# A hand-ordered plan changed: first products of pairs 0 and 1 for both units at once, last halves in two banks, another order of loads

## The chip, the cores and the metric

The kernel runs on one core of a Trainium2 chip. A core has TensorE (matrix products, "PE" in the profile, with its weight loads as "PEld"), VectorE (DVE), ScalarE (ACT), GpSimd (POOL) and SyncE (SP), which here only issues DMAs. The metric is the device time of one execution in microseconds (us); the time before is the median of 3 runs. A profile is one further execution, recorded by the hardware profiler.

## What is computed

A gated linear recurrence (4 batches, 8 heads, 768 steps, head size 48), whose output is at once the input of a two-layer block with SiLU:

```python
f = 1.0 / (1.0 + np.exp(-f_logit))
for t in range(S):
    state = f[:, :, t, :, None] * state + np.einsum('bhd,bhe->bhde', k[:, :, t], v[:, :, t])
    y[:, :, t] = np.einsum('bhd,bhde->bhe', q[:, :, t], state)
x = y.transpose(0, 2, 1, 3).reshape(B * S, H * D)      # 3072 x 384
h = x @ w_in                                           # 384 x 2048
g = h * (1.0 / (1.0 + np.exp(-h)))
return g @ w_out                                       # 2048 x 384
```

All inputs and the output are float32; the kernel computes its products in bf16.

## The kernel before

The 768 steps of a batch are cut into 6 chunks of 128. A *unit* is one chunk of one batch, with all its heads; there are 24. Two units make a *pair*, and there are 12 pairs. Pairs 0 to 3 (form "T") hold the chunks 0 and 1 of one batch, with even and odd steps in the two units; pairs 4 to 11 (form "N") hold the same chunk of two batches.

The program has no loops in the usual sense. PLAN (from line 37) is a list of words, and the last loop (line 510) runs through them and calls `emit`. A word reads `kind.pair.unit...:engine:buffers`. It is put on the queue of the engine named (A ScalarE, V VectorE, G GpSimd, S SyncE, P TensorE). Each engine takes its own words in the order of PLAN and waits, word for word, for what the word needs. So PLAN sets the order on every engine and which buffer is used: PSUM has 8 banks (the number behind P).

The kinds, in the order in which a pair goes through them:

- `f`, `k`, `q`, `v`: loads of the inputs on SyncE's queue (line 241). For T pairs a load has 384 KB; pair 0's f comes in two halves.
- `E`, `L`: exponential and logarithm on ScalarE, together the logarithm of the gate (lines 248, 260, 263). `cs`: its running sum, as a product with a triangle of ones (lines 324, 331).
- `ia`, `a`, `al`: exponentials of that sum (lines 336, 338, 278). `ki`, `qg`: k and q times these (line 341). `vb`: v in bf16 (line 185 or 187).
- `tq`, `qkc`: transposes of q and k on TensorE (line 348) and the copy out of PSUM; later pairs do it with a DMA, `qkD` (line 360).
- `sc`, `at`: the products of q and k within a chunk (lines 369, 373) and the mask over them (line 377).
- `d`, `sd`, `su`: the new state (lines 297, 406, 410, 420). `y`, `yi`: the output of the recurrence (lines 285, 385, 389), `yc` its copy, `yT` with `xc`, or `yD`, its transpose (lines 397, 401).
- `mi.P.j`: two of 16 blocks of 128 columns of the first product for pair P, h = x @ w_in, 6 matmuls (line 271). With a third number only one unit's 128 columns of x are taken, without it both units' 256. `si.P.j`: SiLU of the block on ScalarE (line 276), into hT.
- `mo.P.i.n`: a quarter of the second product for unit i, 4 matmuls of 384 columns (line 306); with a fourth number only one half of the 384 output columns. `oc`: copy out of PSUM. `so`: store (lines 316, 318).
- `wi.n`, `wo.n`: a quarter of w_in or w_out, loaded and cast by a DMA that GpSimd issues (lines 216, 219). wi.n holds the blocks j = 2n and 2n + 1.
- `idle`: matmuls on zeros without use (line 465), which keep TensorE working while it has nothing to do.

ScalarE needs one table of functions for `E`, `L`, `ia`, `a`, `al` and another for `si`; when the kind changes in PLAN, the program loads the other (line 513).

Before the plan's own order starts, its first four loads are issued (line 482), and then masks, ones and zeros are made.

Which buffer a word takes is decided by a name. For `mo` and `oc` it is the pair and the unit, so the two halves of pair 11's output lie in one bank:

```python
if kind == "mo":
    return [("o", *rest[:2])]
```

Of the kernel before, what the change touches and what calls it, by code (L numbers as in the profile page):

```python
# [49 lines left out]
mi.0.1.1:P:0 si.0.3:A:1 mi.0.1.0:P: mi.0.5.1:P: si.1.5:A: ki.3.0:G: mi.0.0.0:P:6 si.0.1:A: mi.0.6.0:P:5 mi.0.0.1:P: su.1.1:G:0 mi.0.7.1:P:4 si.0.0:A:  # L50
mi.0.7.0:P: si.0.2:A: mi.0.6.1:P: ki.3.1:G: mi.1.1.0:P: si.0.6:A: mi.1.7.0:P:0 tq.3.0:P:6 mi.1.7.1:P: qkc.3.0:A:1 mi.0.4.0:P:2 tq.3.1:P:5 si.1.7:A:
mi.0.4.1:P: f.4.0:S:1 mo.0.0.0:P:6 qkc.3.1:A: mo.0.1.0:P:0 si.1.1:A: mi.1.6.1:P:5 si.0.5:A: mi.1.6.0:P: si.1.2:A: mo.1.1.0:P:7 si.1.6:A: mo.0.1.1:P:
si.0.4:A: si.0.7:A: sc.3.1:P:3,1 sc.3.0:P:5,2 at.3.1.0:V:2 vb.2.0:A:4 mo.0.1.2:P: at.3.1.1:V: mo.1.1.1:P: at.3.0.0:V:3 mo.0.0.1:P: q.4.0:S:4
# [56 lines left out]
def kernel(  # L110
# [100 lines left out]
    def emit(kind, rest, eng):  # L211
# [91 lines left out]
        if kind == "mo":  # L303
            cols = part_of(rest[3:])
            for n in range(4 * rest[2], 4 * rest[2] + 4):
                nc.tensor.matmul(at("o", P, i)[:, cols], at("hT", P)[:, n, i * C:(i + 1) * C], w_out_sb[:, n, cols], start=(n == 0), stop=(n == NT - 1))  # L306
# [240 lines left out]
```

## Time and profile before

| | us |
|---|---|
| median of 3 runs (181.39 to 182.42) | 181.42 |
| the profiled execution | 180.93 |
| its span, first to last instruction | 179.2 |

The span is what the views of the trace cover; 1.7 us of the profiled execution lie around it. The page also gives the busy share of each engine in 40 slices of 4.5 us (in tenths, 9 is 90% or more), with what the DMA engines moved:

```profile
PE   6769989999999999999999999999999999999993
ACT  3989983895289999999967558988796991178410
DMA  6999999999999799998478998994994496320043
GB/s 159 324 325 325 240 204 207 199 187 190 242 230 212 92 208 221 168 241 144 84 145 170 188 210 141 252 263 103 179 251 94 97 190 215 88 70 0 0 150 117
```

TensorE is full from the sixth slice on. Its digits in the first five hold the matmuls on zeros too. The DMA engines are full to about 60 us. In views of groups a line reads: source line, engine, operation, output<-inputs, shapes, count | busy us, mean ns of one | idle us just before, and what ended it. In views in order of time the first number is the start, the second the length.

### The profile page before, as it was taken

The page shows a single profiled execution, that of the slowest core. Times are in us where ns is not written, and L with a number is a line of the kernel's source. Part 1 is how long each engine was busy: PE and PEld are TensorE (multiplying, and loading weights), DVE is VectorE, ACT ScalarE, POOL GpSimd, SP SyncE. Part 2 cuts the span into 40 slices and gives each one's busy share as a digit, 9 for nine tenths or more (in the row PEclk, how much of TensorE's full clock was granted, in tenths as well). Part 3 has the DMA queues.
Part 4 walks back from the last instruction along what each step waited for, and adds up shares of the span by engine and source line. Part 5 has one row for each costly group of instructions (what it writes and reads, how often), then busy time and mean ns, then how long its engine had stood idle before and what let it go on. Part 6 is the DMA issues. An engine that isn't in the chain of part 4 may idle for free.

```text
span 179.2 us, 4981 instructions
## 1 busy us (share of the span) xinstructions
PE 170.5 (95%) x2042; PEld 129.0 (72%) x2044; DVE 79.7 (44%) x166; ACT 132.7 (74%) x251; POOL 61.6 (34%) x106
## 2 busy tenths in 40 slices
PE   6769989999999999999999999999999999999993
PEld 2345779975788866778678877875876786788782
DVE  7078994008821246456673703342335747500002
ACT  3989983895289999999967558988796991178410
POOL 6036995000274004554044170636303592000010
...
DMA  6999999999999799998478998994994496320043
GB/s 159 324 325 325 240 204 207 199 187 190 242 230 212 92 208 221 168 241 144 84 145 170 188 210 141 252 263 103 179 251 94 97 190 215 88 70 0 0 150 117
...
## 3 DMA queue, kind: packets, MB, share of 16 engines
...
q14 instruction: 6, 0.05, 0.1%
...
## 4 chain that ended last, share of the span: by engine, by line
PE 77%; ACT 9%; DVE 4%; DMA 3%; SPq 2%; issue 1%; POOL 1%; DVEq 0%
PE pb L306 32%; PE pb L271 32%; ACT hT L276 4%; DMA q<-in_q_dram 3%; PE pb L373 2%; SPq L241 2%; PE pb L385 2%; PE pb L348 2%; PE pb L389 2%; DVE qk L341 2%; ACT L513 1%; DVE atm L377 1%; PE pb L331 1%; PE pb L397 1%; DVE st L420 1%
## 5 line engine op out<-in xcount | busy, mean ns | idle before, releaser
L306 PE MATMUL pb<-w_out_sb,hT 128*128 128x384 bf16 (+1 forms) x416 | 70.4, 314 | 0.2 <-ACT hT L276 0.2
L271 PE MATMUL pb<-xT,w_in_sb 128*128 128x256 bf16 (+1 forms) x672 | 68.9, 257 | 0.0
L271 PEld LDWEIGHTS <-w_in_sb 128*128 128x128 bf16 x672 | 56.6, 98 | 7.5 <-issue 0.3
L276 ACT ACTIVATE hT<-pb 128x512 bf16<-128x512 f32 x96 | 51.8, 617 | 12.4 <-PE pb L271 12.0
L306 PEld LDWEIGHTS <-hT 128*128 128x128 bf16 x416 | 37.7, 98 | 18.7 <-ACT hT L276 0.4
L377 DVE TENSOR_TENSOR atm<-pb,triu 128x512 bf16<-128x512 f32 x32 | 20.6, 684 | 20.5 <-PE pb L373 17.8
L336 ACT ACTIVATE x<-pb 128x384 f32<-128x384 f32 x48 | 22.1, 508 | 1.5 <-PE pb L331 1.4
L420 POOL TENSOR_TENSOR st<-sd,al 48x192 bf16<-48x192 f32 x32 | 16.6, 518 | 18.7 <-PE pb L385 12.1
L341 POOL TENSOR_TENSOR qk<-q,x 128x384 bf16<-128x384 f32 x11 | 11.3, 1025 | 31.9 <-ACT x L336 14.5
L513 ACT ACT_TABLE_LOAD x15 | 19.2, 1283 | 0.3
L185 ACT COPY ob<-pb 128x384 f32<-128x384 f32 (+1 forms) x15 | 6.8, 453 | 12.6 <-PE pb L306 12.6
L377 DVE TENSOR_TENSOR atm<-pb,mask 128x512 bf16<-128x512 f32 x16 | 10.2, 685 | 12.4 <-ACT hT L276 11.1
L187 DVE COPY ob<-pb 128x384 f32<-128x384 f32 (+1 forms) x11 | 5.8, 535 | 22.2 <-PE pb L306 22.2
L318 POOL DMA_DIRECT2D out_dram<-ob x8 | 4.6, 578 | 28.4 <-ACT ob L185 24.8
L316 POOL DMA_DIRECT2D out_dram<-ob x14 | 7.6, 548 | 19.6 <-DVE ob L187 15.9
L341 DVE TENSOR_TENSOR qk<-q,x 128x384 bf16<-128x384 f32 x13 | 7.6, 593 | 13.7 <-ACT x L336 13.7
L248 ACT ACTIVATE e<-f 128x768 f32<-128x768 f32 (+1 forms) x13 | 10.4, 800 | 4.4 <-DMA f<-in_f_logit_dram 4.2
L410 DVE TENSOR_TENSOR sd<-pb,st 128x384 f32<-128x384 f32 x16 | 8.9, 554 | 10.6 <-PE pb L406 3.9
L341 POOL TENSOR_TENSOR qk<-k,x 128x384 bf16<-128x384 f32 x10 | 10.8, 1082 | 6.4 <-ACT al L278 2.0
L185 ACT CAST yb<-pb 128x384 bf16<-128x384 f32 x12 | 5.6, 479 | 9.7 <-PE pb L389 9.6
L341 DVE TENSOR_TENSOR qk<-k,x 128x384 bf16<-128x384 f32 x14 | 9.9, 710 | 0.9 <-ACT x L336 0.9
L187 DVE CAST yb<-pb 128x384 bf16<-128x384 f32 x12 | 6.6, 556 | 8.0 <-PE pb L389 5.9
...
## 6 DMA issues: line engine op xcount, KB each, us to landing
...
```

Of the source, the lines that this page charges most:

```text
L185: nc.scalar.copy(dst, src)
L187: ENG[eng].tensor_copy(dst, src)
L248: return nc.scalar.activation(e, at("f", P)[:, j * w:(j + 1) * w], AF.Exp, scale=-1.0)
L271: nc.tensor.matmul(h[:, i, cols], w_in_sb[:, kk, n * 128:(n + 1) * 128], at("xT", P)[:, kk, cols], start=(kk == 0), stop=(kk == KT - 1))
L276: return nc.scalar.activation(at("hT", P)[:, 2 * j:2 * j + 2, :], at("h", P, j).rearrange("p (n c) -> p n c", n=2), AF.Silu)
L306: nc.tensor.matmul(at("o", P, i)[:, cols], at("hT", P)[:, n, i * C:(i + 1) * C], w_out_sb[:, n, cols], start=(n == 0), stop=(n == NT - 1))
L336: nc.scalar.activation(at(kind, P, i).rearrange("p h d -> p (h d)"), at("cs", P, i)[:, 0:HD], AF.Exp, scale=1.0 if kind == "ia" else -1.0)
L341: ENG[eng].tensor_mul(at("qk", P, i)[:, j, :, 0:D], heads("qk"[j], P, i), at("ia" if j else "a", P, i))
L377: ENG[eng].tensor_mul(at("atm", P, i)[:, r], at(f"s{r}", P, i).rearrange("p (n c) -> p n c", c=C), mask[:, None, :].to_broadcast([C, NP, C]))
L410: nc.vector.tensor_add(at("sd", P, i), d_ps, prev_state(P, i))
L420: ENG[eng].tensor_mul(at("st", P, i)[lo:lo + D, :, r * D:(r + 1) * D], src[lo:lo + D, :, r * D:(r + 1) * D], al_of(P, i)[lo:lo + D, :, Non ...
L513: nc.scalar.preload_act_table_set(TABLES[mode])
```

## The change

PLAN is replaced as a whole; PAIRS, SLOTS and all of the arithmetic stay. Beside it, the name under which the halves of `mo` and `oc` find their bank takes the number of the half, so that a half has a bank of its own:

```diff
@@ emit
-                nc.tensor.matmul(at("o", P, i)[:, cols], at("hT", P)[:, n, i * C:(i + 1) * C], w_out_sb[:, n, cols], start=(n == 0), stop=(n == NT - 1))
+                nc.tensor.matmul(at("o", P, i, *rest[3:])[:, cols], at("hT", P)[:, n, i * C:(i + 1) * C], w_out_sb[:, n, cols], start=(n == 0), stop=(n == NT - 1))
...
-            copy(eng, at("ob", P, i)[:, cols], at("o", P, i)[:, cols])
+            copy(eng, at("ob", P, i)[:, cols], at("o", P, i, *rest[2:])[:, cols])
@@ takes
-            return [("o", *rest[:2])]
+            return [("o", *rest[:2], *rest[3:])]
```

The start of PLAN, to a little past the first product (`mi.0.2.0`):

```diff
-f.2.0:S:0 k.0.0:S:0 f.0.1:S:1 f.0.0:S: E.2.0:A:0 f.1.0:S:2 L.2.0:A:0 v.1.0:S:0 q.0.0:S:0 idle.512.11::0 cs.2.1:P:0 E.0.1:A:1 E.0.0:A: k.1.0:S:1
-cs.2.0:P:1 L.0.1:A:1 L.0.0:A: E.1.0:A:0 q.1.0:S:1 idle.512.1::2 cs.0.0:P:2 cs.0.1:P:3 a.0.0:A:0 vb.1.1:G:0 f.3.0:S:3 L.1.0:A:2 ia.0.1:A:1 cs.1.0:P:4
-a.0.1:A:2 qg.0.0:V:0 v.0.0:S:1 cs.1.1:P:5 ia.1.0:A:3 ki.0.1:V:1 al.1:A:0 ia.0.0:A:4 qg.0.1:V: al.0:A:1 ia.1.1:A:0 k.2.0:S:2 ki.0.0:V: vb.1.0:A:1
-idle.512.4::6 tq.0.1:P:6 ki.1.0:G:2 ia.2.0:A:1 tq.0.0:P:7 qkc.0.1:V:0 a.1.0:A:2 q.2.0:S:2 qkc.0.0:A: qg.1.0:V: ki.1.1:V:3 a.1.1:A:4 idle.512.3::2
-tq.1.0:P:2 q.3.0:S:3 a.2.0:A:3 qg.1.1:G: sc.0.0:P:3,4 qkc.1.0:A:1 sc.0.1:P:6,7 at.0.0.1:V:0 k.3.0:S:3 wi.1:G: at.0.0.0:V: E.3.0:A:1 idle.512.2::5
-tq.1.1:P:5 at.0.1.0:V:1 wi.2:G: d.1:P:1,4 qkc.1.1:A: v.2.0:S:2 su.1.0:V:0 wi.0:G: at.0.1.1:V: al.2:A:2 L.3.0:A:0 idle.512.3::2 sc.1.0:P:2,3 ki.2.0:G:4
-sc.1.1:P:6,1 at.1.0.1:V:2 vb.0.0:A:2 cs.3.1:P:5 vb.0.1:A:3 at.1.1.0:V:3 qg.2.0:G: al.3:A:3 ia.2.1:A:2 d.0:P:7,3 at.1.1.1:V: a.2.1:A:0 cs.3.0:P:6
-ia.3.1:A:4 su.0.0:V:0 qg.2.1:G:2 y.0:P:0,1 a.3.0:A:1 at.1.0.0:V: yc.0.0:A:0 yi.0.1:P: tq.2.0:P:7 a.3.1:A:3 wi.3:G: yc.0.1:V:1 ia.3.0:A:0 y.1:P:0,2
-wo.0:G: ki.2.1:V: yc.1.0:A:2 yT.0.0:P:5 sd.0.1:V:0 yi.1.1:P: yT.0.1:P:1 yc.1.1:A:0 tq.2.1:P:6 xc.0.0:V:0 wo.1:G: xc.0.1:A: qkc.2.0:V:0 v.3.0:S:3
-yT.1.0:P:0 yT.1.1:P:3 xc.1.0:A:1 mi.0.2.0:P:2 qkc.2.1:V: su.0.1:G:0 xc.1.1:A: mi.0.3.0:P:5 mi.1.3.0:P:1 sd.1.1:V:1 mi.1.3.1:P: qg.3.0:V:3 wo.2:G:
-mi.0.2.1:P: sc.2.1:P:7,0 si.1.3:A:0 wo.3:G: qg.3.1:V:0 sc.2.0:P:3,6 at.2.1.1:V:0 mi.1.5.1:P:4 mi.1.2.1:P:1 at.2.0.0:V:1 mi.1.2.0:P: at.2.0.1:V:
...
+f.0.0:S:0 f.0.1:S: f.1.0:S:1 f.2.0:S:2 q.0.0:S:0 E.0.1:A:0 k.0.0:S:0 L.0.1:A:0 E.0.0:A: E.1.0:A:1 k.1.0:S:1 L.0.0:A: L.1.0:A:1 q.1.0:S:1
+idle.512.14::0 cs.0.0:P:0 cs.0.1:P:1 ia.0.0:A:0 E.2.0:A:0 v.0.0:S:0 cs.1.1:P:2 a.0.0:A:1 ia.0.1:A:2 qg.0.0:G:0 v.1.0:S:1 a.0.1:A:3 cs.1.0:P:3
+ia.1.1:A:4 L.2.0:A:2 ki.1.1:V:1 f.3.0:S:3 ki.0.1:V:2 a.1.1:A:1 idle.512.2::4 cs.2.1:P:4 ia.1.0:A:4 ki.0.0:V: cs.2.0:P:5 al.0:A:0 q.2.0:S:2 a.2.1:A:2
+qg.0.1:V: a.1.0:A:0 tq.0.0:P:6 ki.1.0:V:3 al.1:A:1 ia.2.0:A:3 tq.0.1:P:7 qg.1.0:G: k.2.0:S:2 a.2.0:A:4 qkc.0.1:V:0 al.2:A:2 qkc.0.0:A: wi.1:G:
+q.3.0:S:3 vb.1.0:G:0 idle.512.5::0 sc.0.0:P:0,1 sc.0.1:P:3,2 vb.1.1:G:1 at.0.1.0:V:0 E.3.0:A:1 k.3.0:S:3 qg.1.1:G: at.0.0.1:V:1 ia.2.1:A:0 vb.0.0:G:2
+at.0.1.1:V: vb.0.1:A:3 v.2.0:S:2 idle.512.5::5 tq.1.1:P:5 wi.2:G: L.3.0:A:0 at.0.0.0:V: d.1:P:7,6 d.0:P:3,1 qkc.1.1:A:1 su.1.0:V:0 wi.0:G: tq.1.0:P:4
+su.0.0:V:0 qg.2.0:G:4 y.0:P:2,0 qkc.1.0:V: yc.0.0:A:0 yi.0.1:P: cs.3.0:P:7 sd.0.1:V:0 qg.2.1:G:1 yc.0.1:A:1 sc.1.1:P:5,3 v.3.0:S:3 at.1.1.1:V:2
+yT.0.0:P:4 yT.0.1:P:2 xc.0.0:A:0 ki.2.0:G: sc.1.0:P:1,0 at.1.1.0:V: xc.0.1:A: cs.3.1:P:3 a.3.0:A:1 at.1.0.1:V:3 wi.3:G: mi.0.2.0:P:4 a.3.1:A:4
+tq.2.0:P:2 al.3:A:3 at.1.0.0:V: ia.3.1:A:2 ki.2.1:G: mi.0.3.0:P:5 qkc.2.0:A:0 sd.1.1:V:1 mi.0.2.1:P: y.1:P:0,3 wo.2:G: yc.1.0:A:2 yi.1.1:P: tq.2.1:P:1
+yc.1.1:V:0 ia.3.0:A:3 su.0.1:G:0 mi.0.3.1:P: yT.1.0:P:6 yT.1.1:P:2 xc.1.0:V:1 f.4.0:S:0 mi.0.5:P:0 xc.1.1:A: qg.3.1:V:0 wo.0:G: mi.1.4:P:3 qkc.2.1:V:
+wo.1:G: mi.1.5:P:7 si.0.3:A:0 ki.3.1:G: mi.1.2.1:P:6 si.1.5:A:1 mi.1.2.0:P: mi.0.1:P:2 wo.3:G: mi.0.0:P:1 si.0.1:A: si.1.2:A: sc.2.0:P:5,7 si.0.0:A:
...
```

Counted over the whole plan:

| | before | after |
|---|---|---|
| `mi` of pairs 0 and 1, one unit / both units | 32 / 0 | 8 / 12 |
| matmuls on zeros (`idle`) | 24 | 26 |
| changes of ScalarE's table, the first load among them | 16 | 20 |
| `oc` on ScalarE / VectorE | 15 / 11 | 10 / 16 |
| `vb` on ScalarE / VectorE / GpSimd | 8 / 11 / 5 | 5 / 4 / 15 |
| `yc` on ScalarE / VectorE | 12 / 12 | 10 / 14 |
| `xc` on ScalarE / VectorE | 8 / 4 | 6 / 6 |

The second `mo` of pair 0 and 1 also move: before, `y.2` and `d.2` stood behind eleven `mo`; now `y.2` follows the first two (`mo.1.0.0`, `mo.0.0.0`). Around pair 8, `E.10`, `L.10` and `E.11` each stand between SiLUs:

```diff
...
+qkD.9.0:S:3 mo.7.0.2:P: E.10.0:A:0 mi.8.1:P:7 mo.7.1.2:P: so.4.1:S: mo.7.0.3:P: q.11.0:S:1 si.8.1:A:1 mi.8.3:P:1 mi.8.6:P:3 si.8.3:A: f.11.0:S:2
+oc.7.0:A:2 mo.7.1.3:P: si.8.6:A: v.10.0:S: mi.8.4:P:0 oc.7.1:V:3 mo.6.1.3:P: k.11.0:S:5 L.10.0:A:2 sc.9.0:P:7,1 sc.9.1:P:2,3 at.9.1.0:V:2 mi.8.2:P:5
...
+mo.8.1.1:P: yD.9.0:S:1 E.11.0:A:1 y.9.1:P:7 mo.8.0.0:P:5 yc.9.1:V:0 su.9.1:G:0 ia.10.1:A:0 mo.8.0.1:P: yD.9.1:S: L.11.0:A:1 ki.10.1:V:1 mo.8.0.2:P:
...
```

More of the change, by code (lines that the diff above doesn't have):

```diff
@@ L50 @@
[L50 to L53, printed above, removed]
@@ new lines @@
+yc.1.1:V:0 ia.3.0:A:3 su.0.1:G:0 mi.0.3.1:P: yT.1.0:P:6 yT.1.1:P:2 xc.1.0:V:1 f.4.0:S:0 mi.0.5:P:0 xc.1.1:A: qg.3.1:V:0 wo.0:G: mi.1.4:P:3 qkc.2.1:V:
+wo.1:G: mi.1.5:P:7 si.0.3:A:0 ki.3.1:G: mi.1.2.1:P:6 si.1.5:A:1 mi.1.2.0:P: mi.0.1:P:2 wo.3:G: mi.0.0:P:1 si.0.1:A: si.1.2:A: sc.2.0:P:5,7 si.0.0:A:
+at.2.0.0:V:0 mi.1.0:P:2 si.1.4:A: ki.3.0:V:2 mi.1.6:P:6 si.1.0:A: qg.3.0:V: mi.0.6:P:1 si.1.6:A: f.5.0:S:1 at.2.0.1:V: mi.1.1:P:5 si.0.6:A: si.0.2:A:
+tq.3.1:P:3 vb.2.1:G:4 tq.3.0:P:2 qkc.3.1:A:1 vb.2.0:G:5 mi.1.3.0:P:6 qkc.3.0:V: mi.0.4:P:7 si.1.1:A: mi.1.3.1:P: si.0.5:A: mi.0.7:P:1 si.1.3:A:
@@ new lines @@
+mi.2.5:P:0 L.5.0:A:2 k.5.1:S:5 sd.3.1:V:0 yi.3.1:P: yc.3.0:V:0 mo.1.1.1:P: yc.3.1:A:1 q.6.1:S:0 oc.1.0:A:1 yT.3.0:P:2 mo.1.1.2:P: xc.3.0:V:3
+cs.4.0:P:7 mi.2.1:P:4 a.4.0:A:0 ia.4.0:A:4 qg.4.0:V:3 cs.4.1:P:3 k.7.1:S:0 yT.3.1:P:5 ki.4.0:V: mi.2.0:P:2 xc.3.1:A: a.4.1:A:2 v.4.1:S:4 mi.3.4:P:5
+al.4.0:A:4 al.4.1:A:5 ia.4.1:A:3 mo.1.1.3:P: v.4.0:S: mi.3.7:P:7 oc.1.1:V:2 qg.4.1:V:1 si.2.1:A:2 mi.2.6:P:3 ki.4.1:V: si.3.4:A:3 tq.4.0:P:1 si.2.6:A:
+qkD.4.1:S:0 mi.2.7:P:4 qkc.4.0:A:1 mi.3.1:P:5 vb.4.1:G:3 f.6.0:S:3 si.2.5:A: mi.2.4:P:3 v.5.1:S:5 si.2.0:A: mi.2.2:P:1 si.2.4:A: mi.3.5:P:0 si.2.7:A:
@@ new lines @@
+cs.8.1:P:0 yc.5.1:V:0 mo.4.0.1:P: al.7.1:A:5 ia.7.1:A:3 yD.5.0:S:1 a.7.1:A:4 vb.7.1:V:0 mo.4.0.2:P: ia.8.1:A:1 qg.7.1:G:4 d.6.0:P:3 a.8.1:A:2
+d.7.0:P:4 sd.6.0:V:0 yT.5.1:P:2 qkc.6.0:A:1 mo.4.0.3:P: q.9.1:S:3 ki.7.1:V: mo.4.1.1:P: a.8.0:A:0 qkD.7.1:S:2 ia.8.0:A:4 mo.4.1.2:P: al.8.1:A:2
+xc.5.1:A: ki.8.0:G:0 oc.4.0:A:1 sc.6.0:P:3,1 sc.6.1:P:0,2 al.8.0:A:0 at.6.0.0:V:1 so.3.0:S: d.7.1:P:6 mi.5.5:P:5 sd.7.0:V:1 k.8.1:S: at.6.0.1:V:
+mi.5.4:P:3 f.9.0:S:1 at.6.1.0:V:0 mi.5.2:P:4 qkD.7.0:S:3 qg.8.1:V:3 mi.5.6:P:1 si.5.2:A:0 at.6.1.1:V: si.5.5:A: mi.5.0:P:0 si.5.6:A: y.6.0:P:4
```

95 lines of the change are left out of this document (42 added, 53 removed).

## The prediction

> **What bounds the kernel now.** I read the page first, then the waits of TensorE, then the chain of waits in order of time, then the timeline of the first 24 us.
>
> ```profile
> span 179.2 us, 4981 instructions
> PE 170.5 (95%) x2042; PEld 129.0 (72%) x2044; DVE 79.7 (44%) x166; ACT 132.7 (74%) x251; POOL 61.6 (34%) x106
> PE 77%; ACT 9%; DVE 4%; DMA 3%; SPq 2%; issue 1%; POOL 1%; DVEq 0%
> ```
>
> TensorE (PE) is busy 95% of the span and is 77% of the chain that ends last. Its matmuls overlap, so busy is not peak; what it waits for says more. The view of waits, for TensorE from 20 us to the end, holds two rows (total us, times, longest):
>
> ```profile
> PE pb L369 <- issue: 0.9, 1, 0.9
> PE pb L306 <- ACT hT L276: 0.2, 1, 0.2
> ```
>
> So from 20 us on TensorE stands for 1.1 us in all. Whatever the new order does there, it can win little; it can only lose. Time can be won ahead of the first product, which starts at 23.58 us, and by making the products cheaper. The chain of waits around that point:
>
> ```profile
> 21.37 0.45 PE pb L348 x8
> 21.82 0.52 PE pb L285 x32
> 22.34 0.27 PE pb L397 x3
> 22.61 0.17 PE pb L385 x4
> 22.79 0.17 PE pb L397 x3
> ...
> 23.74 1.68 PE pb L271 x30
> 25.42 0.45 PE pb L369 x21
> 25.87 0.85 issue
> 26.72 0.36 PE pb L369 x11
> 27.08 7.48 PE pb L271 x132
> ...
> 155.22 8.52 PE pb L271 x78
> ```
>
> These rows give prices on the path: a product of 128 columns costs 7.48/132 = 56.7 ns, one of 256 columns 8.52/78 = 109.2 ns, a set of eight transposes (tq, L348) 0.45, a y of a T pair (L285) 0.52, a yi (L385) 0.17, a yT (L397) 0.17. The wait of 0.9 is the row of 0.85 "issue", inside the two sc of pair 2 (32 small matmuls in one burst).
>
> What holds the first product? The timeline of the start:
>
> ```profile
> 4.05 0.84 ACT L248 ACTIVATE e<-f 128x768 f32<-128x768 f32 x1 [2.03 <-DMA f<-in_f_logit_dram]
> 4.92 0.84 ACT L260 ACTIVATE lf<-e 128x768 bf16<-128x768 f32 x1
> 8.90 0.50 POOL L187 CAST vb<-v 128x384 bf16<-128x384 f32 x1 [4.98 <-DMA v<-in_v_dram]
> 10.14 0.56 DVE L341 TENSOR_TENSOR qk<-q,x 128x384 bf16<-128x384 f32 x1 [5.93 <-ACT x L336]
> 14.89 1.00 POOL L341 TENSOR_TENSOR qk<-q,x 128x384 bf16<-128x384 f32 x1 [2.39 <-ACT x L336]
> 15.83 2.46 POOL L216 DMA_DIRECT2D w_in_sb<-in_moe_w_in_dram  x3
> 16.70 1.03 ACT L185 COPY qkTT<-pb 128x1024 bf16<-128x1024 bf16 x1
> 19.38 1.64 ACT L336 ACTIVATE x<-pb 128x384 f32<-128x384 f32 x4
> 22.38 0.97 ACT L185 CAST yb<-pb 128x384 bf16<-128x384 f32 x2
> 23.24 1.25 ACT L185 COPY xT<-pb 128x384 bf16<-128x384 bf16 x3
> 23.58 1.84 PE L271 MATMUL pb<-xT,w_in_sb 128*128 128x128 bf16 x30
> ```
>
> ScalarE (ACT) works nearly without a break from 4.05. Its steps cost 0.84 for a whole E or L, about 0.38 for an exponential ((1.64 less one latency of 0.5) / 3), 1.03 for a qkc, 0.48 for a yc. In the plan of before, five E, five L, 16 exponentials, 4 small al, 3 qkc, 3 vb and 3 yc stand ahead of xc.0.1: 8 x 0.84 (four pairs, E and L) + 16 x 0.38 + 4 x 0.2 + 3 x 1.03 + 6 x 0.48 = 19.6 us; from 4.05 that is 23.6, and its copy xT ran at 23.24. The count fits, so ScalarE's queue sets the first product. The weights are the second holder:
>
> ```profile
> DMA to landing us min/median/max: 7.4/9.5/11.0
> ```
>
> Of the four loads of w_in the quickest took 7.4 us. The first was issued at 15.83, so it landed at 23.2 or later, 0.3 us ahead of its use.
>
> **The change part by part.**
>
> *Order led by pair 0.* The new plan has ahead of xc.0.0 the same E and L, but 12 exponentials, 3 al, 2 qkc, 1 vb and 2 yc: 6.7 + 4.6 + 0.6 + 2.1 + 1.4 = 15.4, so ScalarE could come to it at 4.05 + 15.4 = 19.5, 4 us earlier, if it never waits. It waits: walked step by step, qkc.0.0 is done at 14.3, the four masks of pair 0 (DVE) end at 17.5, y.0 ends at 18.7, yT.0.0 stands on TensorE behind sc.1.1, which waits for qkc.1.0 on DVE until 19.6, and xc.0.0 ends at 20.8. First product at 21.1 by that walk. Are the inputs there? From f.2 (first load, 4.05) to q.0 (sixth whole load, used at 10.14) a load takes (10.14 - 4.05)/5 = 1.2 us; v.1, the fifth, fits at 8.90. In the new order q.0 is the fourth (7.7), k.1 the sixth (10.1), v.1 the ninth (13.7); only f.3 (14.9) comes as late as it is asked for, a wait of half a microsecond which lies in the walk.
>
> *Weight loads.* On POOL's queue wi.1 now follows qg.0.0 and qg.1.0. qg.1.0 needs a.1.0, which ends on ScalarE at about 12.7 (4.05 + 3.4 for two whole E and L pairs, 1.7 for the halves, 9 x 0.38, 0.2), and takes 1.0 on POOL: issued at 13.7 in place of 15.83. At 7.4 us it lands at 21.1, at one more input load ahead of it in the same engines at 22.3. I take a first product at 21.7, 1.9 us earlier. [...]
>
> *What goes behind the first product.* Ahead of it the new plan no longer has tq.2.0 and tq.2.1, y.1, yi.1.1 and the two yT of pair 1: 2 x 0.45 + 0.52 + 0.17 + 2 x 0.17 = 1.93 us of TensorE's work. It is done later, on the path. So the 1.9 earlier and the 1.9 more come to nothing: that is the core of this forecast. The masks of pair 1 end near 22.6 on DVE, when TensorE has done three half products and tq.2.0, so y.1 costs a wait of 0 to 0.3; in the sum it is 0.1.
>
> *The burst of sc.* sc.2.0 and sc.2.1 stood together right behind the first products, and there lay the 0.85 that no record explains. Now sc.2.0 stands alone some ten products later, and sc.2.1 between the two sc of pair 3. The wait goes (-0.85) or moves with the next burst (0); I take -0.5.
>
> *wi.2.* The first whole product, mi.0.5, needs the second load. Between wi.1 and wi.2 POOL now does vb.1.0, vb.1.1, qg.1.1 and vb.0.0 (0.5 + 0.5 + 1.0 + 0.5), so wi.2 is issued at 13.7 + 0.8 + 2.5 = 17.0, later than before (15.83 + 2.46/3 = 16.65). TensorE comes to mi.0.5 at 21.7 + 4 x 0.34 + 1.93 = 25.0. Landing after 7.4, 9.5 or 11.0 us gives 24.4, 26.5 or 28.0: a wait of 0, 1.5 or 3.0. The load ahead of it in the queue is issued 2 us earlier than before, so the engines come to this one sooner than to the median one, and I take a landing near 25.3, between the first two: 0.3. All that is queued behind mi.0.5 on TensorE waits with it, and nothing else: the SiLUs start only after a table load.
>
> *Merged products.* In pairs 0 and 1, 12 of 16 blocks now run for both units.
>
> ```profile
> L271 PE MATMUL pb<-xT,w_in_sb 128*128 128x256 bf16 x480 | 57.3, 272 | 0.0
> L271 PE MATMUL pb<-xT,w_in_sb 128*128 128x128 bf16 x192 | 11.5, 219 | 0.0
> L513 ACT ACT_TABLE_LOAD x15 | 19.2, 1283 | 0.3
> L185 ACT COPY ob<-pb 128x384 f32<-128x384 f32 x12 | 5.8, 486 | 4.9 <-PE pb L306 4.9
> ```
>
> Of the 192 small matmuls 144 become 72 of 256 columns: 72 x (2 x 56.7 - 109.2) = 0.3 us less. That is small because TensorE's time goes with columns, not with instructions; the 72 weight loads that go lie under the matmuls already.
>
> *Two banks for the last halves.* While a half is copied, TensorE fills the other half. TensorE has no wait in the end of the trace (the two rows above are all), so the second bank takes nothing off it: 0. The last copy goes from ScalarE to DVE, for 192 columns a difference of some 0.05, taken as 0.
>
> *Rest of the plan.* The plan has four more changes between the exponential and the SiLU table (20 for 16): 4 x 1.28 = 5.1 us on ScalarE; it gives away 5 oc, 3 vb, 2 yc and 2 xc, 12 x 0.48 = 5.8 at most. ScalarE stays at 74%. On TensorE: 0 at best (two rows, 0.2 us), up to 3 us of new waits (below). I take 0.2.
>
> Sum: -1.9 + 1.93 + 0.1 - 0.5 + 0.3 - 0.3 + 0.2 = -0.2, no change. The profiled execution took 180.93 (the span of 179.2 and 1.7 around it), so 180.7 of the new one; the median of the runs is 181.42, half a microsecond above the profiled one, which gives a median of 181.2.
>
> **The rivals.**
>
> *Faster.* The weights are not in the way: the first product starts at 21.1 (-2.5), no wait for wi.2, the 0.85 gone whole. -2.5 + 1.93 + 0.1 - 0.85 - 0.3 = -1.6, and with xc.0.0 a microsecond sooner than the walk has it -2.6: from 181.42, 178.8 to 179.8. For it: ScalarE has 4 us less ahead, and wi.1 comes 2 us earlier. Against it: 7.4 us is the quickest of four landings.
>
> *Slower by table changes.* The new plan goes to the exponential table and back three times within the products of pair 8 and around them (E.10, then L.10, then E.11). Each visit keeps ScalarE from SiLUs for 2 x 1.28 + 0.84 = 3.4 us, in which TensorE can fill 3.4/0.66 = 5 banks of 8. Where the plan has no mo to put between, TensorE stands; a microsecond a visit gives +3 and 184.4. It decides once fewer than 3.4 us of mo, y and sc stand between two SiLUs. Against it: the plan of before has such visits already, and TensorE waited 0.2 us.
>
> *Slower by late inputs.* Weights that start 2 us earlier share the engines earlier with q.3, k.3, v.2 and v.3. How they share, from 24 to 30 us:
>
> ```profile
> q0 software_dynamic: 907, 0.86, 85.8%
> q1 hardware_dynamic: 907, 0.34, 33.2%
> ```
>
> Packet for packet, so inputs move at 0.34 MB in 6 us, where alone 384 KB take 1.2. Two microseconds of full speed lost are some 0.55 MB, which then lands up to 9.6 us later. v.2 is asked for by y.2, now two mo behind the first mo. If v.3 lands after 45 us, TensorE waits: +2.5, 183.9. Against it: both plans have to move the same bytes by then. [...]
>
> **How the numbers follow.** About 1% (1.8 us) is what a measurement of this kernel can tell from no change. No change 0.47 (own range 179.7 to 183.2), faster 0.25, slower by tables 0.17, slower by inputs 0.11. The range that leaves out a tenth at either end is 178.6 to 184.3.
>
> **What would show it.** Right: the first L271 at 21 to 22.3 us, with tq, y and yT among the first products; the waits of TensorE after it naming w_in's load for 0 to 1.5 us; 600 matmuls on L271. Wrong: a first L271 after 23, waits on ScalarE's SiLUs around pair 8 of over a microsecond, or on v.2 or v.3; or an end of the start-up so early that over 1.8 us are won.

## The result, and the profile after

| | before | after |
|---|---|---|
| median of the runs, us | 181.54 (181.39 to 182.42, 4 runs) | 183.79 (183.00 to 184.96, 4 runs) |
| ratio to before | | 1.012, 95% interval 1.008 to 1.016 |
| profiled execution, us (span) | 180.93 (179.2) | 184.37 (182.6) |

The change made the kernel slower, by 1.2%; the prediction said no change (-0.2 us). The profiled execution of after is 3.4 us longer than that of before, and 0.6 above the median of after. The ratios, and the counts of executions further down, leave out single executions that took over 1.5% longer than the fastest of their kernel; the medians hold them. In the kernel after, every line from the changed ones on has a number 2 lower (L271 is L269, L348 is L346).

The page, of after (span; engines; the chain that ended last, by engine and by line):

```profile
span 182.6 us, 4867 instructions
PE 172.0 (94%) x1974; PEld 127.2 (70%) x1974; DVE 81.7 (45%) x169; ACT 133.4 (73%) x243; POOL 65.8 (36%) x116
PE 75%; DMA 12%; SPq 8%; DVE 1%; issue 1%; POOL 1%; DVEq 0%; POOLq 0%
```

TensorE is as busy as before, but DMA has gone from 3 to 12% of the chain. The waits of TensorE after 20 us (total us, times, longest), of after:

```profile
PE pb L346 <- POOL qk L339: 2.0, 2, 1.5
PE pb L269 <- DMA w_in_sb<-in_moe_w_in_dram: 0.5, 1, 0.5
PE pb L269 <- DMA xT<-yb: 0.5, 1, 0.5
```

That is 3.0 us where before had 1.1. The largest is on GpSimd's products for the transposes; the chain says what those waited for (start, us, what):

```profile
16.83 17.77 DMA k<-in_k_dram
...
34.77 1.28 POOL qk L339
...
36.09 0.40 PE pb L346 x4
```

The k load of pair 3 was issued at 16.83 and took 17.8 us; before, no k load took more than 6.2 us. The timeline of TensorE has the first product and the first whole one:

```profile
22.50 0.49 PE L269 MATMUL pb<-xT,w_in_sb 128*128 128x128 bf16 x6
27.22 4.12 PE L269 MATMUL pb<-xT,w_in_sb 128*128 128x256 bf16 x42 [0.51 <-DMA w_in_sb<-in_moe_w_in_dram]
```

The first product is 1.08 us sooner than before (23.58), not 1.9. So this one profile told of a tidy cause: weights 1.3 us earlier (issued at 14.50 for 15.83), the k load behind them, a wait of 1.5 us at the transposes of pair 3 (some of the expectations below count it as 1.8). The experiments show that the loss does not rest on it.

### The profile page after: what moved, and what is told of

Read it like the earlier page. It is cut to its first block, busy times and chain, and to the rows that moved or that the text cites. A ratio compares the mean times of both kernels' runs of the same rounds, so it can differ in the third digit from the quotient of the medians.

```text
span 182.6 us, 4867 instructions
## 1 busy us (share of the span) xinstructions
PE 172.0 (94%) x1974; PEld 127.2 (70%) x1974; DVE 81.7 (45%) x169; ACT 133.4 (73%) x243; POOL 65.8 (36%) x116
## 4 chain that ended last, share of the span: by engine, by line
PE 75%; DMA 12%; SPq 8%; DVE 1%; issue 1%; POOL 1%; DVEq 0%; POOLq 0%
PE pb L304 33%; PE pb L269 30%; DMA k<-in_k_dram 10%; SPq L239 8%; PE pb L371 2%; DMA xT<-yb 2%; PE pb L383 2%; PE pb L387 2%; PE pb L329 1%; PE pb L404 1%; PE pb L346 1%; PE pb L395 1%; POOL qk L339 1%; DVE yb L185 1%; PE pb L332 1%
## 5 line engine op out<-in xcount | busy, mean ns | idle before, releaser
L269 PE MATMUL pb<-xT,w_in_sb 128*128 128x256 bf16 (+1 forms) x600 | 70.5, 268 | 1.0 <-DMA w_in_sb<-in_moe_w_in_dram 0.5
L269 PEld LDWEIGHTS <-w_in_sb 128*128 128x128 bf16 x600 | 54.9, 97 | 10.2 <-DMA xT<-yb 0.8
L304 PEld LDWEIGHTS <-hT 128*128 128x128 bf16 x416 | 38.0, 97 | 17.8
L185 DVE COPY ob<-pb 128x384 f32<-128x384 f32 (+1 forms) x16 | 8.3, 516 | 34.8 <-PE pb L304 34.8
L334 ACT ACTIVATE x<-pb 128x384 f32<-128x384 f32 x48 | 21.3, 503 | 1.4 <-PE pb L332 1.4
L185 POOL CAST vb<-v 128x384 bf16<-128x384 f32 x15 | 7.3, 503 | 27.8 <-DMA v<-in_v_dram 27.6
L316 POOL DMA_DIRECT2D out_dram<-ob x9 | 5.1, 566 | 24.0 <-DVE ob L185 24.0
L246 ACT ACTIVATE e<-f 128x768 f32<-128x768 f32 (+1 forms) x13 | 10.2, 791 | 4.5 <-DMA f<-in_f_logit_dram 4.5
L339 POOL TENSOR_TENSOR qk<-k,x 128x384 bf16<-128x384 f32 x8 | 8.2, 1032 | 14.4 <-DMA k<-in_k_dram 5.9
L375 DVE TENSOR_TENSOR atm<-pb,mask 128x512 bf16<-128x512 f32 x16 | 10.2, 683 | 5.6 <-PE pb L367 3.3
L185 DVE CAST yb<-pb 128x384 bf16<-128x384 f32 x14 | 7.7, 555 | 9.6 <-PE pb L387 5.1
L463 PE MATMUL pb<-zero,triu 128*128 128x512 bf16 x26 | 9.0, 504 | 1.4 <-POOL triu masks.py:66 1.4
L346 PE MATMUL pb<-ident,qk 128*128 128x128 bf16 x80 | 6.5, 220 | 2.4 <-POOL qk L339 2.3
```

The lines of the kernel that those rows point to most:

```text
L185: ENG[eng].tensor_copy(dst, src)
L246: return nc.scalar.activation(e, at("f", P)[:, j * w:(j + 1) * w], AF.Exp, scale=-1.0)
L269: nc.tensor.matmul(h[:, i, cols], w_in_sb[:, kk, n * 128:(n + 1) * 128], at("xT", P)[:, kk, cols], start=(kk == 0), stop=(kk == KT - 1))
L304: nc.tensor.matmul(at("o", P, i, *rest[3:])[:, cols], at("hT", P)[:, n, i * C:(i + 1) * C], w_out_sb[:, n, cols], start=(n == 0), stop=(n ...
L334: nc.scalar.activation(at(kind, P, i).rearrange("p h d -> p (h d)"), at("cs", P, i)[:, 0:HD], AF.Exp, scale=1.0 if kind == "ia" else -1.0)
L339: ENG[eng].tensor_mul(at("qk", P, i)[:, j, :, 0:D], heads("qk"[j], P, i), at("ia" if j else "a", P, i))
```

## The experiments

Ratios are to runs of the kernel before on the same chip. Each kernel is the kernel after with the edit shown, unless it is said to start from before. In the plan's words, a line with - is the order that goes and one with + the order that comes.

**Less weight traffic.** Each of the eight weight loads brings a quarter of its columns or rows; the rest of the weights is zero, so the products are of other numbers. Two more fills of zeros, for the second weights, on GpSimd and VectorE, are not printed.

```diff
-nc.gpsimd.dma_start(out=w_in_sb[:, :, n * w:(n + 1) * w], in_=w_in_src[:, :, n * w:(n + 1) * w])
+nc.gpsimd.dma_start(out=w_in_sb[:, :, n * w:n * w + w // 4], in_=w_in_src[:, :, n * w:n * w + w // 4])
...
+nc.vector.memset(w_in_sb, 0.0)
```

> The changed kernel with each of the eight weight loads cut to a quarter (the rest of the weights is zero, so three quarters of both products are computed on zeros). Theory L (the weights' loads, issued earlier, hold back the loads of k.2, k.3, v.2 and v.3): TensorE's waits for k (2.0 us) and for w_in (0.5) go, k.3 lands by 24 us instead of 34.6, and the time falls by 2.5 to 3.5 us against the changed kernel, to about 180.5. Rival O (the order on the queues of GpSimd and ScalarE makes the waits, whatever the DMAs do): the waits before tq.2.0 and tq.3.1 stay, less than 0.7 us is won.

The same cut in the kernel before:

> The same cut of the weight loads in the kernel before (three quarters of the weights are zero). Theory L: its inputs for pairs 2 and 3 landed in time, so little is won, 0 to 1.2 us (the 0.9 us wait without a record may go with it). If both kernels with cut loads take the same time within 0.5 us, all of the slowdown is the meeting of weights and inputs; if the changed one stays 1 us or more slower, something in the order itself costs it.

Measured: after with a quarter 182.0 us (ratio 1.0015, 0.9985 to 1.0045); before with a quarter 183.29 (1.0047, 1.0012 to 1.0082). The k loads, of after with a quarter (DMA to landing, shortest, median, longest):

```profile
DMA to landing us min/median/max: 3.3/4.2/6.4
```

So it is the weights that make the k load late: 6.4 us at most without three quarters of them, 17.8 with them. The waits for k and for w_in are gone as theory L had it, but only 1.3 to 1.8 us are won, not its 2.5 to 3.5. That before grew slower with less traffic was expected by no theory. Two things are seen. The fills of zeros hold VectorE for 2.6 us from 7.3 and 1.3 from 10.2, and the first product starts at 26.4. And TensorE's granted clock, 0.997 or more in nearly all executions of before, was 0.99 in 7 of 10: these took 183.21 to 183.54 us, the three with the full clock 182.15 to 182.52. So about 1 us of it goes with the clock.

**The weights later, one input earlier.**

```diff
-wi.1:G: q.3.0:S:3 vb.1.0:G:0 ... vb.1.1:G:1 ... qg.1.1:G: ... vb.0.0:G:2 ...
+q.3.0:S:3 vb.1.0:G:0 ... vb.1.1:G:1 ... qg.1.1:G: ... vb.0.0:G:2 wi.1:G: ...
```

> The changed kernel with wi.1 moved on GpSimd's queue from behind qg.1.0 to behind vb.0.0, right ahead of wi.2. Theory L: k.3 is issued ahead of all weights, lands by 25 us, the wait before tq.3.1 (1.8 us) goes; but wi.1 lands 2 us later, the first product starts at 24 to 24.5 instead of 22.5 and has more done ahead of it, so the total moves by -1.5 to +0.5 us. Rival O: the wait before tq.3.1 stays at 1.5 us or more and the later first product is lost on top: +1 to +2 us.

```diff
-v.0.0:S:0 ... v.1.0:S:1 ... f.3.0:S:3
+f.3.0:S:3 v.0.0:S:0 ... v.1.0:S:1 ...
```

> The changed kernel with the load of f.3 moved ahead of v.0 and v.1 on SyncE's queue. ScalarE waited 1.6 us for f.3 at 15.2 us with everything for pair 0 queued behind it. If that wait sets the first product, it starts 0.8 to 1.5 us earlier and the total falls by 0.5 to 1 us. If theory L holds and k.3 decides, the first product comes earlier but the wait before tq.3.1 grows by as much, and the total stays within 0.4 us of the changed kernel.

Measured: 184.7 us (1.0151, 1.0106 to 1.0197) and 182.7 (1.0031, 0.9999 to 1.0064). With the weights later the wait for k is gone, no k load takes more than 6.1 us, and the kernel is as slow as ever: the first product waits for the weights and starts at 25.8. The two transfers trade places. With the f load early the time is 0.6 to 1.1 us below after's, but not by an earlier first product: in its one profile that starts at 24.2, later than in either profile of after.

**Both kernels a second time; the late step moved.**

> The kernel after the change, unaltered, a second time with a profile. If the loss comes from inputs that share the engines with weights 2 us earlier, the same waits of TensorE stand there again: tq.2.0 on the k load of pair 2 (0.3 to 0.8 us), the first whole product on w_in (0.3 to 0.8), tq.3.1 on the k load of pair 3 (1 to 2.5), with the first product at 22.2 to 23.2 us; and the stream of inputs runs at 215 to 250 KB a microsecond between 3 and 6 us, as in the first profile. If the wait of 1.8 us was an accident of one execution, it is under 0.5 here, at the same time of the whole within half a microsecond.

> The kernel before, unaltered, a second time with a profile, to see what of its start is steady. If the order of the loads sets the rate of the early stream, it moves 320 KB or more a microsecond from 3 to 6 us again, and the first product starts at 23.3 to 23.9. If the rate is chance, it differs by tens of KB from the first profile in that stretch.

```diff
-tq.3.1:P:3 ... tq.3.0:P:2 ... mi.1.3.0:P:6 ... mi.0.4:P:7 ... mi.1.3.1:P: ... mi.0.7:P:1 ... sc.3.1:P:4,3 sc.2.1:P:2,5 sc.3.0:P:0,6 ... mi.1.7:P:7
+mi.1.3.0:P:6 mi.0.4:P:7 ... mi.1.3.1:P: ... mi.0.7:P:1 tq.3.1:P:3 tq.3.0:P:2 ... mi.1.7:P:7 sc.2.1:P:2,5 sc.3.1:P:4,3 sc.3.0:P:0,6
```

> The kernel after with the transposes of pair 3 behind four more products (4.0 us of TensorE's work) and the last product of pair 1 and the scores of pair 2 between them and the scores of pair 3; nothing else is moved. If what is lost at 34 us is only that the k load of pair 3 lands late and TensorE stands in front of its transposes, the wait of 1.8 goes, at most 0.4 comes back at the scores of pair 3, and the time is 1.2 to 1.8 us below the kernel after: 182.0 to 182.6. If the next late input takes its place (the v loads of pairs 2 and 3 land behind it), TensorE waits as long a few products later and the time is within half a microsecond of the kernel after, 183.3 to 184.3.

Measured: after again 183.29 us (1.0069, 1.0033 to 1.0105); before again, one run of 181.34; the transposes of pair 3 later 183.87 (1.0086, 1.0043 to 1.013). With the transposes moved, the wait for k is gone from the profile, four shorter waits (1.5 us in all) stand there instead, and the time has not fallen. And in the second profile of the unaltered kernel there is no such wait at all; TensorE's waits after 20 us:

```profile
PE pb L383 <- DVE st L418: 0.5, 1, 0.5
PE pb L269 <- DMA xT<-yb: 0.4, 1, 0.4
```

That execution took 182.56 us, still 1.2 above the second profile of before. Its first product starts at 23.62, no sooner than before's (23.58 and 23.75). What it has instead is seen in the windows of one microsecond (busy time of the engines with the number of instructions, granted clock of TensorE, DMA share, GB/s), of the second profile of after:

```profile
9.00:10.00 1.00, 1.00 (x14) 0.59 (x13) 0.00 (x0) 1.00 (x3) 0.00 (x0) 1.00 0.89 195
10.00:11.00 1.00, 0.19 (x1) 0.00 (x0) 0.00 (x0) 1.00 (x4) 0.85 (x1) 1.00 1.06 278
11.00:12.00 1.00, 0.01 (x1) 0.01 (x1) 0.26 (x1) 1.00 (x3) 0.14 (x1) 1.00 1.16 321
12.00:13.00 1.00, 1.00 (x12) 0.65 (x12) 1.00 (x3) 0.93 (x4) 0.00 (x0) 0.71 1.16 323
13.00:14.00 1.00, 1.00 (x11) 0.88 (x9) 1.00 (x3) 1.00 (x4) 0.16 (x1) 0.50 1.14 308
14.00:15.00 1.00, 1.00 (x10) 0.98 (x10) 0.18 (x1) 1.00 (x4) 1.00 (x2) 0.50 1.06 280
15.00:16.00 1.00, 0.78 (x4) 0.32 (x3) 0.69 (x1) 0.67 (x1) 1.00 (x3) 0.58 1.13 295
16.00:17.00 1.00, 1.00 (x35) 0.56 (x33) 0.00 (x0) 0.05 (x1) 1.00 (x3) 1.00 1.16 323
```

From 10 to 12 us TensorE works 0.2 us in all: behind the second group of fillers it waits 1.8 us for the logarithm that the sums of pair 2 need. Then, just as the work comes, its clock is granted at half speed for 3.4 us. The first profile has the same wait (first its row in the timeline of TensorE, then windows) and keeps the clock:

```profile
11.75 0.48 PE L322 MATMUL pb<-lf,tincl 128*128 128x384 bf16 x2 [1.80 <-ACT lf L258]
```

```profile
10.00:11.00 1.00, 0.00 (x0) 0.00 (x0) 0.00 (x0) 1.00 (x4) 0.90 (x1) 1.00 1.02 277
...
13.00:14.00 1.00, 0.93 (x14) 0.64 (x12) 0.76 (x3) 1.00 (x4) 0.60 (x1) 1.00 1.16 323
```

What differs between the two can be read from the clock records of the 20 profiles. Counted from the start of the full clock, it changed in them only after whole multiples of 3.41 us. In seven profiles it fell in the start, each time behind a stretch of 3.41 us in which TensorE was busy for 1.08 to 1.63 us; behind a stretch with 1.81 us or more it fell in none. In the second profile of after one stretch holds the whole wait; in the first a border at 10.31 cuts the wait in two (windows, the second profile and then the first):

```profile
9.01:12.42 3.41, 1.61 (x21) 0.88 (x19) 0.68 (x2) 3.33 (x8) 1.00 (x1) 1.00 1.05 271
```

```profile
6.90:10.31 3.41, 2.68 (x28) 1.47 (x27) 0.00 (x0) 3.41 (x8) 0.40 (x1) 1.00 1.05 287
10.31:13.72 3.41, 1.90 (x28) 1.45 (x28) 2.43 (x5) 3.41 (x10) 0.91 (x2) 1.00 1.14 316
```

So the order brought the wait in both executions, and where the borders lay, 9.01 and 12.42 us in one and 6.90, 10.31 and 13.72 in the other, went with the fall. That the work within such a stretch decides is the author's reading of these profiles; what sets the borders is not shown.

The mean granted clock stands beside every timed execution, so it can be counted. Half speed for 3.4 of some 181 us is a mean of 0.99. Of the timed executions 5 of 124 of before are below 0.995, and 10 of 13 of after. In the chain of the second profile of after (start, us, what; L463 are the filler matmuls on zeros, L346 the transposes):

```profile
13.32 1.71 PE pb L346 x16
...
15.25 1.32 PE pb L463 x4
16.57 0.57 PE pb L367 x32
17.14 1.19 PE pb L463 x5
```

The 16 transposes of pair 0 take 1.71 us, where the prediction had 0.9 (0.45 for eight), and the fillers that stand behind them, meant for a wait, have come late and now stand on the chain themselves.

**What holds the start?** Four ways to move it.

```diff
-f.0.0:S:0 f.0.1:S: f.1.0:S:1 f.2.0:S:2 q.0.0:S:0 ... k.0.0:S:0
+f.0.0:S:0 k.0.0:S:0 f.0.1:S: f.1.0:S:1 q.0.0:S:0 f.2.0:S:2
```

> The kernel after with two loads moved: the k load of pair 0 goes second and the q load of pair 0 ahead of the f load of pair 2, so that no more than two f loads follow each other. If it is the row of f loads that slows the early stream, it moves 300 KB or more a microsecond from 3 to 6 us (215 to 250 in the kernel after), the eleventh load of 384 KB is in 0.5 to 0.8 us sooner, and the first product starts up to 0.7 sooner: 183.0 to 183.6. If the halved first load or chance slows it, the rate stays at 215 to 250 and the time is 183.5 to 184.5, since the f loads of pairs 1 and 2 now come later.

```diff
-idle.512.2::4 ... idle.512.5::0 ... idle.512.5::5
```

> The kernel after without its three later groups of filler matmuls on TensorE (2, 5 and 5 of 512 columns, results unused), the last two of which stand ahead of the scores of pair 0 and of the second transposes of pair 1. In the second profile of the kernel after, where the inputs come later than planned, both groups of 5 lie on the chain that leads to the first product, at 1.32 and 1.19 us, although what they stand ahead of was ready 0.4 to 0.8 us sooner. If they hold the first product, it starts 0.4 to 1.2 us sooner than in that profile (at 22.4 to 23.2 us) and the time falls by as much: 182.1 to 182.9 against 183.3. If they only fill waits, the first product stays where it is (23.2 to 23.8) and the time within 0.3 us; if TensorE's clock falls further without them, the granted clock from 9 to 18 us is below the 0.7 to 0.8 of that profile and the time is above 183.6.

```diff
-ki.1.1:V:1 ... ki.0.1:V:2 ... cs.2.1:P:4 ... ki.0.0:V: cs.2.0:P:5 ... qg.0.1:V: ... tq.0.0:P:6 ... tq.0.1:P:7 ... sc.0.0:P:0,1 sc.0.1:P:3,2
+ki.0.0:V:0 ki.0.1:V:2 ... qg.0.1:V: ki.1.1:V:1 ... tq.0.0:P:6 tq.0.1:P:7 cs.2.1:P:4 ... cs.2.0:P:5 ... sc.0.1:P:3,2 sc.0.0:P:0,1
```

> The kernel after with the products of pair 0 ahead of the one of pair 1 on VectorE, their transposes ahead of the sums of pair 2 on TensorE, the copy of the transposes on ScalarE ahead of three small steps of pair 2, and unit 1 of pair 0 first in the scores. So pair 0 no longer waits for the k load of pair 1, the sixth load, which came at 11.3 to 11.7 us where the walk had 10.1. If that late load is what puts off the first product, the masks of pair 0 end 1 to 2 us sooner and the first product starts 0.7 to 1.3 us sooner than in the second profile (22.3 to 22.9): 182.0 to 182.6 us. If the queue of GpSimd holds it (the issue of the first weights, two casts, then the last q product of pair 1, which ends at 17.4 to 17.9), the masks end sooner all the same, the first product starts at 23.1 or later, and the time stays within 0.4 us of 183.3.

```diff
-qg.1.0:G: ... wi.1:G: ... vb.1.0:G:0 ... vb.1.1:G:1 ... qg.1.1:G:
+qg.1.1:G: qg.1.0:G: ... wi.1:G: ... vb.1.0:G:0 ... vb.1.1:G:1
```

> The kernel after with one step of GpSimd moved: the second q product of pair 1 goes ahead of the first, into a wait of 2.5 us, instead of behind the issue of the first weights and two casts. If GpSimd's queue holds the first product, the second transposes of pair 1 follow the filler at once and the first product starts 0.4 to 0.9 us sooner than in the second profile of the kernel after (22.7 to 23.2): 182.4 to 182.9 us. If the masks of pair 0 hold it, the first product stays at 23.2 or later and the time within 0.3 us of 183.3; it is worse, by up to 1.8, where the second weight load, now issued a microsecond sooner, gets ahead of the k load of pair 3 and TensorE waits for that again.

| | us | ratio, interval | clock below 0.995 |
|---|---|---|---|
| loads mixed | 183.23 | 1.0047, 1.0011 to 1.0082 | 6 of 9 |
| three filler groups out | 183.65 | 1.0102, 1.0052 to 1.0152 | 4 of 4 |
| pair 0 first | 182.83 | 1.0042, 1.0006 to 1.0077 | 1 of 10 |
| q product of pair 1 first | 183.93 | 1.0106, 1.0078 to 1.0135 | 9 of 9 |

Without these fillers the mean granted clock of the profile is 0.972, where the second profile of after has 0.988 (windows of the kernel with three filler groups out):

```profile
13.00:16.00 3.00, 1.51 (x17) 1.04 (x20) 2.10 (x4) 2.90 (x9) 1.93 (x2) 0.66 1.04 264
16.00:18.00 2.00, 1.02 (x32) 0.78 (x32) 0.86 (x2) 0.54 (x1) 2.00 (x4) 0.50 0.98 252
18.00:21.00 3.00, 2.87 (x45) 2.53 (x46) 2.64 (x6) 2.73 (x5) 2.98 (x5) 0.50 1.06 190
21.00:24.00 3.00, 3.00 (x61) 1.95 (x60) 1.67 (x5) 0.92 (x2) 1.00 (x2) 0.50 1.20 255
```

The rival held here: the clock fell further and nothing was won by the fillers that no longer stood in the way. "Pair 0 first" is the one of the four that gives TensorE work in the wait (0.8 us from 10 to 12 us, for 0.2), and the one that keeps the clock. Its median is half a microsecond or more below after's, but the intervals overlap, and with the full clock in 9 of 10 executions it is still 0.4% slower than before. Moving the load order or GpSimd's product won nothing that can be told from after's 183.3 to 183.8.

**The wait filled.** Only the fillers change here, whose results nothing reads.

```diff
-idle.512.14::0 ... idle.512.2::4
+idle.512.17::0 ... idle.512.10::4
```

> The kernel after with more filler matmuls on TensorE: 17 in place of 14 ahead of the first sums and 10 in place of 2 ahead of the sums of pair 2, 0.6 and 1.7 us at 0.21 each, to cover the waits of 1.2 and 1.8 us that stand behind them; nothing else. If TensorE's clock halves early on because it stands still there, the mean granted clock is 0.997 or more in at least 8 of 10 executions (3 of 14 in the kernel after), the first product starts at 22.3 to 23.0 us, and the time falls by 0.4 to 1.2 us: 182.2 to 183.0 against 183.3 to 183.8; it falls no further since with an early start the k load of pair 3 comes too late again. If the clock has nothing to do with those waits, it stays at 0.99 in most executions and the time does not change by more than 0.3.

> a_fill unaltered, with more rounds, to set its time against the kernel before more closely. If the fillers give back the whole loss, the ratio to before is within 0.3% of 1 (181.1 to 182.0 us); if the change is worth something beside its loss, it is below before by 0.3 to 0.8%; the granted clock is 0.997 or more in nearly all executions.

Before, without its last four groups of fillers (4, 3, 2 and 3 of them):

> The kernel before without its four later groups of filler matmuls (4, 3, 2 and 3 of 512 columns, results unused, between 10.5 and 18 us); the first two groups stay. If the fillers keep TensorE's clock up in before, the mean granted clock falls to 0.97 to 0.99 in most executions (0.997 or more in nearly all with them) and the time rises by 0.5 to 1.8 us: 182.3 to 183.6. If before does not need them, since its inputs come steadily, clock and time stay (181.3 to 182.0).

| | us | ratio, interval | clock below 0.995 |
|---|---|---|---|
| after, wait filled | 181.69 | 1.0011, 0.9982 to 1.0040 | 0 of 9 |
| the same again | 181.77 | 0.9979, 0.9944 to 1.0014 | 0 of 10 |
| before without fillers | 181.96 | 1.0045, 1.0015 to 1.0075 | 9 of 10 |

The windows of after with the wait filled, against the eight above:

```profile
10.00:11.00 1.00, 1.00 (x7) 0.45 (x5) 0.00 (x0) 1.00 (x4) 0.94 (x1) 1.00 1.15 320
11.00:12.00 1.00, 0.97 (x6) 0.39 (x5) 0.97 (x3) 1.00 (x3) 0.00 (x0) 1.00 1.17 320
...
13.00:14.00 1.00, 1.00 (x16) 0.76 (x14) 0.74 (x2) 1.00 (x4) 0.57 (x1) 1.00 1.14 315
```

Eleven matmuls on zeros give the loss back, more than the 0.4 to 1.2 us expected, and taking such matmuls out of before costs it 0.45% (0.6 us by the medians of that chip, of the 0.5 to 1.8 expected). Both directions agree, so this much is shown: the loss hangs on these matmuls on zeros in the start.

That they act through the clock is shown for before without fillers. There the clock sorts the ten executions: 180.96 us at 1.0, 181.57 to 181.82 at 0.991, 182.11 at 0.981, 182.38 to 183.49 at 0.969 to 0.972. For after the clock alone is not enough. Its ten executions below 0.995 took 182.27 to 184.96 us, with a median of 183.1; its three with the full clock took 183.19, 183.59 and 184.37. And the second profile with the wait filled, at the full clock, has its first product at 23.43, only 0.2 us sooner than the second profile of after, while its span is 1.0 shorter (179.8 for 180.8). More than half of that arises at 155 us, at the first product of pair 10 (TensorE; second profile of after, then the second with the wait filled):

```profile
154.92 0.81 PE L304 MATMUL pb<-w_out_sb,hT 128*128 128x384 bf16 x4
156.12 1.16 PE L269 MATMUL pb<-xT,w_in_sb 128*128 128x256 bf16 x9 [0.38 <-DMA xT<-yb]
```

```profile
154.49 0.81 PE L304 MATMUL pb<-w_out_sb,hT 128*128 128x384 bf16 x4
155.13 2.13 PE L269 MATMUL pb<-xT,w_in_sb 128*128 128x256 bf16 x18
```

After waits here for the DMA that transposes y (3.9 us; in the two profiles of the filled wait none after 148 us took over 3.2). This is the row "DMA xT<-yb" in both lists of waits above. It stands in nine of the ten profiles of after and its variants without the filled wait, and in none of the six with it. How fillers at 10 us change a transfer at 152 us is not shown.

**On top of the filled wait.** With the transposes of pair 3 later (as above); with "pair 0 first" and six fillers in the second group, and those transposes later; with the f load of pair 3 early; and with the 12 merged blocks of pairs 0 and 1 run for each unit again:

```diff
-mi.0.5:P:0 ...
+mi.0.5.0:P:0 mi.0.5.1:P: ...
```

> a_fill with the transposes of pair 3 four products later, as in a_tq3_late. If the clock and the late k load are the two halves of the loss, taking both away gives 181.6 to 182.4 us, and the profile has a first product at 22.3 to 23.0 and no wait for the k load over 0.3. If the late inputs only pass on to the v loads and the output weights, it is no better than a_fill.

> a_ki0 with 17 and 6 filler matmuls in the first two groups (its wait behind the second is shorter) and the transposes of pair 3 four products later. If the causes add up, it is 0.3 to 0.8 us below a_ki0's 182.8: 182.0 to 182.5, with the full clock in all executions. If the transfers of the first 45 us set a floor under all of these orders, it stays at 182.5 to 183.0, with new short waits for v or the output weights.

> a_fill with the f load of pair 3 ahead of the v loads of pairs 0 and 1, as in a_f3_early: weights go out about a microsecond later against the inputs, so the k load of pair 3 is in on time, and the wait of ScalarE for f goes; the v loads come a load later and put off the first product. If the late inputs behind the first product are still worth more than that, it is 0.3 to 0.8 us below a_fill (180.9 to 181.4); if the first product decides, it is 0.3 to 1.0 above (182.0 to 182.7).

> a_fill with the 12 merged blocks of products of pairs 0 and 1 run for each unit by itself again: 72 products of 256 columns become 144 of 128, as the kernel before has them; the order stays. The prediction's term for the merging is 0.3 us (72 times twice 56.7 less 109.2 ns): if it holds, this kernel is 0.1 to 0.5 us slower than a_fill, and TensorE's time from its first product to the last product of pair 1, without waits, is 0.3 longer. If the weight loads that come back do not hide under the shorter products, it is slower by a microsecond or more.

Measured: 181.84 us (1.0024, 0.9991 to 1.0057), 182.43 (1.0062, 1.0039 to 1.0084), 181.99 (1.0005, 0.9972 to 1.0037) and 182.71 (1.0043, 1.0009 to 1.0076). None beats the filled wait alone, and none beats before. The causes do not add up: moving the transposes is worth nothing here either. The split is 0.9 to 1.0 us slower than the filled wait, more than the 0.3 expected. The chain of the two, from mi.0.5 on (five merged blocks and two half ones), first as they are in the second run of the filled wait, then split:

```profile
26.94 4.02 PE pb L269 x42
```

```profile
27.15 3.47 PE pb L271 x60
```

30 merged and 12 single products take 4.02; 60 single ones take 3.47, which makes 72 take 4.16: 0.14 more for 30 of the 72 merged products, so 0.3 for all, the term as it was forecast. (This kernel's lines are numbered as before's.) The rest of the microsecond is not explained by the products; its profile has a wait of 0.4 us for the k load of pair 3, and that is one execution.

## Why the prediction was wrong

**First product at 21.7 instead of 23.58 (-1.9).** This is the step that failed: 22.50 in one profile and 23.62 in the other, so -1.1 and 0.0. The second is past 23, which the forecast itself had named as a sign of being wrong. What it had wrong is the price of a load, 1.2 us each. The walk had the k load of pair 1 at 10.1; VectorE's first product, which needs it, started at 11.27 in the first profile of after and at 11.74 in the second:

```profile
11.27 1.50 DVE L339 TENSOR_TENSOR qk<-k,x 128x384 bf16<-128x384 f32 x3 [7.06 <-DMA k<-in_k_dram]
```

```profile
11.74 1.50 DVE L339 TENSOR_TENSOR qk<-k,x 128x384 bf16<-128x384 f32 x3 [7.52 <-DMA k<-in_k_dram]
```

From there to the first product the walk had 11.0 us (10.1 to 21.1). In all seven profiles that keep after's order up to there, fillers aside, and the full clock it is 11.2 to 11.4 (22.50 less 11.27 in the first). So the steps of the engines were priced well, and the loads that they start from came 1.2 to 1.6 us late. In the second profile it is 11.9: there the clock adds some 0.6, and the chain goes back to the f load of pair 1, which landed at 6.6, where 1.2 us a load from 4.05 make it 5.25. The first weights were issued at 14.50, where the sum had 13.7.

Counted over the packets of the trace, the six whole loads' bytes that end with this k load are in at 10.1 to 11.2 us in every profile that keeps after's order of the first loads; in the three of before's order without another edit the sixth is in at 9.6 to 9.7. The second whole load takes 1.4 to 1.8 us in after's order. Why this order moves slower stays open; the mixed order of loads sped it up in part and won no time.

**The fillers and the clock.** The forecast did not name the filler matmuls, although the plan's two counts of them (24 and 26) stood beside the diff: two more in all, but 14, 2, 5 and 5 in place of 11, 1, 4, 3, 2 and 3, with a bare wait of 1.8 us behind the 2. The granted clock was in the page, at 9 in every slice of before, and it was read as a constant of the chip, where it differed between orders and, in the two profiles of after, between executions of one program (a mean of 1.000 and 0.988). What the eleven more are worth: 183.29 or 183.79 less 181.69 or 181.77, 1.5 to 2.1 us, which would have made the forecast of no change right, with a first product still at 22.4 to 23.4.

**How the sum closes.** The second profiles of after and before have spans of 180.8 and 179.6, 1.2 apart. The terms as measured there are -0.1 for the first product (23.62 for 23.75), +1.9 for the work behind it, -0.85 for the scores, -0.3 for the merging, and 0.55 for the stop at 155 us: 1.2. So the first product's term is 1.8 short of the -1.9 in the sum, and the term of 0.2 for new waits was 0.35 too small.

**More work behind the first product (+1.93).** Right: of the matmuls ahead of it 48 transposes of q and k have become 32, 64 of y 32, 8 of yi 4 and 12 of yT 6, which is 1.9 us at the forecast's prices. **Wait for y.1 (+0.1).** None over 0.1 in either profile; in the first the transposes of pair 2 beside it waited 0.5 for their k load.

**Wait for wi.2 (+0.3, 0 to 3.0).** Right in size: 0.5 in the first profile, none in the second.

**The burst of scores (-0.5).** The row "issue" of 0.9 is gone from the waits of both profiles of after: -0.85, the better of the two ends.

**Merged products (-0.3).** Right, by the rows above. **Two banks (0).** TensorE has no wait in the last products; from the start of its last matmul to the end 3.4 us pass, where before had 3.2. The two banks were not tried alone. **Rest of the plan (+0.2).** The wait for the transpose of y at 155 us, 0.4 to 0.5 in both profiles, is new, and the forecast did not have it. ScalarE's further table changes hold nobody: no wait of TensorE on a SiLU over 0.2 us in either profile, so the rival of the table changes is out.

**The rival of late inputs.** Its mechanism is real: weights that started earlier made inputs late (a k load of 17.8 us in the first profile, 6.4 at most with a quarter of the weights), and the first profile paid 2.0 us for it, near the 2.5 of the rival, at the k loads of pairs 2 and 3 and not at v. But it shows in one of two profiles, and taking its wait away won nothing. That its sum, 183.9, is near the measured 183.79 is luck: the second profile has none of these waits, and the filled wait gives the loss back with k loads that still take up to 15.2 us. The rival "faster" needed a first product at 21.1 and fell with the same step. **What stays open:** three of after's 13 executions kept the full clock and still took 183.2 to 184.4 us. One of them is the first profile, with the late k load; the other two have no profile. Open are also the slower loads at the start and the way from the fillers to the wait at 155 us.
